# A planned attention and MoE kernel: key and query groups of four banks in place of six, with another list of ranks

## The chip, the cores and the metric

The kernel runs on one core of a Trainium2 chip. The metric is the device time of one execution in microseconds. Three runs of the kernel before took 358.09, 358.15 and 360.07, with a median of 358.15.

## What is computed

The reference is a linear attention with learned features, followed by a two-layer product with an ELU. Cut to what matters:

```python
def phi(x):                                   # x: 8 batches, 8 heads, 576 rows, 64 columns
    proj = x @ w_phi                          # 64 -> 128 features
    proj = proj - max(abs(proj), axis=-1)
    return concat([exp(proj), exp(-proj)])    # 256 features

q_p, k_p = phi(q), phi(k)
kv = einsum('bhsf,bhsd->bhfd', k_p, v);  z = sum(k_p, axis=2)
x = einsum('bhsf,bhfd->bhsd', q_p, kv) / (einsum('bhsf,bhf->bhs', q_p, z) + 1e-6)
x = x.transpose(0, 2, 1, 3).reshape(4608, 512)
h = x @ w_in                                  # 512 -> 2048
out = where(h > 0, h, exp(min(h, 0)) - 1) @ w_out   # 2048 -> 512
```

## The kernel before

**Tiling.** The attention works in 16 quads: quad `i` is half of batch `b = i // 2`, that is four heads. Of the 576 rows of a head, 512 are the main part and 64 the tail. For each quad TensorE projects the transposed keys and queries by `w_phi` (L689 for the main part, L671 for the tail), and projects the queries again with the features on the partitions (L864 and L876). The main projections contract over 64 rows only, so two heads run side by side on the two row halves of the array (`project_halves`, L689, and `queries_f`, L864). VectorE takes the largest absolute value of every row (L710), and ScalarE takes the exponentials straight from the projections (`EK` L757, `Eq` L944). GpSimd scales the values by the keys' weights (L808, L818). TensorE makes `kv` (L992) and the outputs (L1046, L1060, L1074). VectorE sums them (L1095, L1101) and GpSimd divides (L1143, L1172).

The MoE part works in nine chunks of 512 tokens. Chunk 0 needs quads 0 and 1; chunks 1 to 7 need two quads each; chunk 8 is made of all the tails. Each chunk has 16 first products (`ph`, L1354 in chunk 0, L1339 after), the ELU in three steps (ScalarE `e_sb` L1367, GpSimd `u_sb` L1371, VectorE `gT` L1383, the last of which reads `ph` again), and 16 second products (`po`, L1443), which are copied (L1471) and stored (L1480, L1484). The last pieces of chunk 8 are 256, 128 and 128 columns wide and share one buffer in SBUF.

**Order of the work.** The kernel is straight-line code, and a planner writes its order when the program is built. `plan_quad`, `plan_chunk` and `plan_loads` hand in operations with an estimated cost, what each depends on, and the PSUM banks that it takes (`new`) and reads (`uses`). There are eight banks, of four kinds: "first" for projections and transposes, "second" for `kv` and outputs, "ph" and "po" for the MoE part. `Planner.run` steps through a modelled time; each time an engine is free, it starts the ready operation with the lowest rank whose banks are free. The ranks stand in `RANKS`, two characters an operation, in the order in which the operations were handed in. An operation of mode 1 (the matmuls over 64 rows) after one of mode 0, or the reverse, costs a planned 0.095 us more (`CHANGE`). In the first 60 planned microseconds a gap of TensorE is half filled with matmuls on zeros (`fill`, L1651). What the chip runs is the resulting fixed order of each engine, with semaphores.

**Around the change.** For batches 4 to 7 (`b > MERGED`, `MERGED = 3`) the main keys and the first half of the first form of queries are one operation on TensorE: `keys` writes four banks of keys and two of queries. The other queries are one operation as well, `others`: the second half of the first form and both halves of the second form, six banks. For batches 1 to 3 keys are one operation of four banks, and for batches 2 and 3 each half of the queries is one operation of four banks (`both`). Quad 0 and 1 have smaller ones. In `run`, `first` is the lowest rank of the ready operations of more than four banks that don't find their banks free; no operation of a higher rank may take a bank ahead of it.

The queries of batch 0 are loaded in two halves by GpSimd (heads 0 to 3, heads 4 to 7), as are its keys and values; GpSimd also issues the loads of `w_in` (two) and `w_out` (four), and from quad 5 on SP issues the transposes of keys and queries by DMA.

Of the kernel before, what the change touches and what calls it, by code (L numbers as in the profile page):

```python
# [34 lines left out]
    "0t12141E1R1T8c1U1b6-1H1M1Q1Y1O1f1V1X1Z1k1m1q1u1g1v1r1i1x221tNx4iOS4-074Q7UBL0587"  # L35
    "4k6J2O5m2w2u5S2r2s5P2i2h5R2e2d5T2n2f2m2g1j1l1n251o47480A2A8KBQAx9591920b415A5B8G"
    "8E998z5D4o9698869B9ADU9RDS8J3z5t4M3X7J2t3c7H743o9M5EDV4w759t0p0n9z5i5h5u094F4R3+"
    "3w1+6N0J4Z066P0U8-04A+FHB0BP7l7mBJ8U7vBM7w8TBK7y7xBN8v7u8Y8Z612620272GAfAg3fDR5M"
    "586a6b6Z9kDQDNAKAJ9N8yAv8x5J4n90Aq9QAy97Aw2EB46f2o2q3k0O5p6C2p3v352J6QKM3t6FKN6W"
    "4K4IIu6l6rIt6q4T5H4e4Y4t0m2K2ZBR6OEy0200BZ5+7C3d5z6m4U7N3h3rAs4N9D0-6+7Q2F664u9y"  # L40
    "5W6I5G5o6S7dNk1h6x5F9v4DBd724G9L8n4d13DE931DAu4L4q107KAU446e0o3IA-5gC3EC235C3KC-"
    "7c0HBG55602YRGBD4jA69j3VE39C9V6BCH7P4EANEpC6DhD82XBUATFTFZ6tJl7L9s8b8iAZ4a2bAFB2"
    "7I1W4v4W9I1e4V8M3H338Q2D2C8L322x8F3834494J4H2+2y2P5Z5a5X5Y5c5b0y0r5v5w3Y3a3Z3b1c"
    "0w3B3A3l3i3m3j2v8f4g4f4h2cD42aDD534O9e3xBaAD1s0s0e3sBhBc5-8HBF363130ARClE1EW6R9+"
    "B57V2V9m4XCO01595l77715j7670659-736K9o786n2z39A29n8k1715161G8V8W2l3yABAC7GCL7FCK"
    "2-1a0v0u5e5Q5d5U3W0d0j0l0k54At689d9uDeE6AQEVDL4SBnBl9wE5DYAGDfCn6j1z1yGR4ABiAiFY"
    "3q63AMII1J6H0T5N1S4m1BGy0q691CGX8N8q198ICI037MAn9PJQ6pBw9l3n3EGoHHCD0xFt2WDWI5FF"
    "0f52JDBt6wAeID84Dz3-MDBC6g9rIAB67k6MFm4bF54lIEA5BxCMCFMiEEDHFsA7Ci0XB9FvGdCdDMEZ"
    "9F7-CV89FULg5r24212Q1-6i9S3J5V5q9g3e5k5n6G37ALBfB-C0BeD9CQBmCRCTBgDADCAO9K9JD6D7"
    "3C3G3D3F0c0i0h3pCkCjCgChCbCc406467CwC+CvCz5sBu9W9XCyAXBHBkC74z0+0BGW1F0C4y0E08Eb"  # L50
    "0g1ABj9xAP185x5yB7F4Co0aDT1d46ASAl8u8jAo8l8dAm8m8sAp8w8eDJCeCf8t8rA9626L6D6EA8AY"
    "4pCYBy1L1K1N1I4x6u6s9b9q9c9p6zAc8P8O2UEL6dEc8+BrIFIB8R454sBpKkHWBqH6MBBs42I4N32N"
    "2MBAB8GSMJEiHiEYPvAaH-EeEuFSVuCEWJC2ESCUWFB3ENCSW6BWGmCJTOBTIQCNBv94GgCPI34cETBO"
    "VQ6hHE7XVEF+Es51B17SAW3gEnK2VxDXW3EMWGD5U-DwVhD3ThC4VsDcEKDkD0S7IzDZEJDdFQVpJ3FO"
    "FMFIFgAbEkEFGpGqH19HEj5f6v3T6oAIEaAkEOMuJm5I4+0Z0K7j0V280N0W2H0L0Y0M0I0z1P0Q2I29"
    "Ds3SDm3Q3R3NDv5KGcGb7g7i7h825LGtGu8p8h7Y8BAr0P2L2T8o8aMl88IYEdGrNM7BQ3Ms7sH4Hq7r"
    "H3Ho7AQ2Mr505657AH1pJkJtG6F343CmMC6U6XNn6V7+Np808DMQ816T4r2S2R8C2B3U3L3MHZHa3P3O"
    "85TeTdRlM5M4Rj5OSfSgA1A3A4A09GFd7z7tRz7DNBC9LvBEJcEQBIOYEU7RJZGl7TFoGhCCJXERV+4C"
    "4B6kBSDjVLQCMyDFU0V-6cBbVqNRBV9OU+VNHTFVPeAERfFETWGCRTEPT1AhSzEGT2DbGTE9SFL5G3Ga"
    "TpIVI9FnSxFfH8GHRiAjI-FlGzFaIkFzJ-C1HsFkCGPtHnFi7EFXEDFwFxPIKVHgBzHNMFM6KZIZL9Hy"  # L60
    "KCMLPoKBFpEwGYEmJCLdGM0D0G3u0F0R0SDiBB9f9ECW7eWYWQWaWXWPWbWgWdWNWfWeWcMVNGNFWkWm"
    "W0WVWTWRWUWSWWWOWZ8XWMWLWoWiWKWhWpWsWqWrDOWjWlWnSQ9UTv9TVrF7SB79F9Rh7OF8HGRgF2HF"
    "7aF1HJ7bReCsCtD2Bo6Y8S6y7WDlCaVVV4V3VzV0W4VyUzV5VOV2VKVwW2W1W5VSV1L3L2L4L1VvVtW7"
    "VWEIDKDIWBWAVnW9W8VmWCWE7ZEHVeVgWHD-TwE0T3FLGEG5FNG4HdFyHhHzEzGkHfE8UpUwGGCpCqEX"
    "B+JLIPQIITJ7I8J6LqIaIjAVLQHlIqS6KKJVJgN6HQJRJaN0IHIXHOS5H+JHLbKSHVExO-KrJJEvPgKG"
    "MRG0QOOALWHbPULsSbGJQlHpStH5ULDgQKLIShMgRsKRHmLURwGKFBLaLnQQKYJBKcKaLcKlNtP9O1Oz"
    "PDGwJNHKP4KHMxMvJp6A2j1w2kJECZDqH2E4HPE7FPUZSrSsUPSqSnUOSoSmUaTUSy8AQzWITSTQJzJ+"
    "JuJwJxJyJvUQUNEoUqUoTmTlTqTrToUEUAUCD+83THTLU9GN7nGO7fJIIGG-GQGvI6HkCXKDIWJ4G+JK"
    "LoKnGLKTKUE+E-IvIoJ1DGHjFDGxIgIiHIIdJnISIfINHDIMIeGFTnU8JYIhS4KsKXKWL6N2N5H9HAGP"
    "G1G2GiGjGBGDGAG9G7G8FhHt7o7pIOEtMnFGQZHXSuRXFCM8SLLJRvSwLKRtUFGIS0UKDBFJFKKFJFKq"  # L70
    "UnNqPJOVTkRBR4KLSeTPMGK1SEUrLhK3JdTJMeK8M1SULlKAEqUJLiK0J2UTKhK9STU7LxHvTNPZO8Fu"
    "TIMHRpHrR2TZRqMwTGTKOZMXT8KOO5O0SWAzMKMqScPVSKFjPRRDNAS+RENLR8QqRIQ+GVMdJUJbNEQ0"
    "RkJqPGPEQTQRFrErBYC5BXKoUlDPCBAd7qDaI0TFNJP7TDPiPBTBP5PATCP6PhLtJfJjPnPmOBOJOKOI"
    "ONOCOMTETAF6U2U3P+PsPrQfQhQrQVQgElMNPkPjQWLMKdLLKmK5MtKyIJOLKPK7NoLZK4LpKwK+VDVX"
    "LyU6UUNlRMKtLPKuKpJhHYVoU4UgVfUmUfVaUhUbVcUdUeSpURUSTaVRTYTXUWUXUVUYU5VbVdHcViVj"
    "VZVYVMVGVHVJVIVFKbVBTMT-T7HSRrHURyKxRSRPKzRRSANIRQS2KeSOS8NHS1TfIL9Z9YLeGUP3JGGf"
    "QSNeQ69hN1QXJ5J0M7QsR-LfMUQmPOLuNyRAQjFRO2R1NQPyL-QuRKSRHCR6OWPFDnRUPqOUGZNYOyEf"
    "N9SjPlFeKiSdIsPCSHSkOmN8KESYNjNrR5OuPzOaFASlSaOtLFFbM+LELSLTNUHxRFNXNaNhNiOlRWOR"
    "OQOXOTIRMILBCuCACrOFQHFqF0FWFcHLLCV7UBT9V6T4T6VAUsTgVCUvT5RuUyUxU1R3TjTyTxTiTzUM"
    "T+V9V8IKVTVUTbTcTuUjUkTsTtUiNmUIVlVkKvMzSSMAUHImPWQaIlPSQbIpQGQdInQcQFJTQtRoQeEB"  # L80
    "EAHeGnNuO3LAKILVMhQpRdRnP1RcRYQoRNRaP2RmRZSJUGUDQLQMDxDuDpE2DtDrDyQnP0NDSXSZIwJ9"
    "IxJ8I+JAIyQ8NdQYQNQ5Q9N7SVN4ROQvMYNgRCM9LmR7MWMSQUMcMTQkMbMPDoEhEgPwPYI7NPRbM0K6"
    "SGL+PHLGI2OsLkLDRJJePuLRM3SNSPNWN+S9NOLXLrF-JsLjQJJiQ7NZIrLOM-NcMERLNvNVMoHRS3NT"
    "GeGsMaNbNCNsPxOOQiS-N-ODOrR0OvOPRHNSSiKgK-L0OeNNNwOdOxPbOiOnOqQDUtR9WDJrNKICI1HB"
    "IcRxPMKjLwPTLNOfOpO7UcOEQ4LYMmObNfJoSIOhQ-O4KQOcQAQBSCOgTRT0O9PaKfQxMMO+NzMpRVPd"
    "PpD1OGPcO6L8MfOwLzOjOHUuR+OkP8TTPLQEMOSvKJSDJSTVQPPQPXH0HMIUIbPfQw9aAAC8CxQyP-L7"
    "LHM2MjPPOoHuHwPKMZJMJOJPJWPNMk4P9i8g11Q1VPH7SM"
# [37 lines left out]
class Planner:  # L125
# [43 lines left out]
    def run(self):  # L169
# [8 lines left out]
        mode = 0  # L178
        pending = []
        landed = []  # L180
        DONE = len(self.ops)
# [55 lines left out]
        while todo:  # L237
            started = False
            for e in ready:
                if free[e] > now:  # L240
                    continue
                best = None
                first = min(
                    [o.rank for at, o in ready[e]
                     if at <= now and len(o.new) > 4 and not fits(o, e)],
                    default=DONE,
                )
                for at, o in ready[e]:
                    if at > now or o.engine or not fits(o, e):
                        continue  # L250
                    if o.new and o.rank > first:
                        continue

                    if any(
                        c < o.cost[e]
                        and free[x] <= now
                        and not any(a <= now and y is not o for a, y in ready[x])
                        for x, c in o.cost.items()
                    ):
                        continue  # L260
                    if best is None or o.rank < best.rank:
                        best = o
# [64 lines left out]
def kernel(  # L327
# [31 lines left out]
    MERGED = 3  # L359
# [162 lines left out]
    def plan_quad(i):  # L522
# [198 lines left out]
        for cs in ((0,), (1,), (2,)) if i == 0 else ((0, 1), (2,)):  # L721
            tail = cs == (2,)

            with_q = b > MERGED and not tail
            if with_q:
                q_first = [Bank("first") for _ in range(2)]

            def keys(e, cs=cs, with_q=with_q):
                for c in cs:
                    project_halves(0, range(4 * c, 4 * c + 4), main_banks[c])  # L730
                if with_q:
                    project_halves(1, range(4), q_first)

            new = [tail_bank] if tail else [x for c in cs for x in main_banks[c]]

            o = add(
                {"PE": 0.11 if tail else 0.22 * (len(cs) + with_q)},
# [3 lines left out]
                [moved[0][-1] if tail else moved[0][cs[0]], *old("kv"), landed["w_phi"]]  # L741
                + ([moved[1][0], *old("out")] if with_q else []),
                new=new + (q_first if with_q else []),
# [103 lines left out]
        exps_q = []  # L847
        m_qs = {0: [], 1: [], 2: []}
        for c in range(3):
# [4 lines left out]
            if b > MERGED and c == 0:  # L854
                pair = q_first
# [30 lines left out]
            if c < 2 and b > MERGED:  # L886
                if c == 0:
                    o, o_f = ops["k"][0], None
                    ops["q"].append(o)
                    rest = [(queries_f, pair_f)]  # L890
                else:
                    rest = [(queries, pair), *rest, (queries_f, pair_f)]

                    def others(e, rest=rest):
                        for f, _ in rest:
                            f(e)

                    o = o_f = add(
                        {"PE": 0.66}, others, deps,
                        new=[x for _, p in rest for x in p], mode=1, key=key,  # L900
                    )
            elif c < 2 and b > 1:
# [15 lines left out]
            if o_f:  # L918
                ops["q"] += [o] if o is o_f else [o, o_f]
# [768 lines left out]
```

## Time and profile before

| | us |
|---|---|
| median of three runs | 358.15 |
| the profiled execution | 358.15 |
| its span on the core | 356.4 |
| TensorE busy | 344.2 |
| VectorE busy | 264.4 |
| ScalarE busy | 261.6 |
| GpSimd busy | 243.5 |
| `po` L1443, 584 matmuls | 133.0 |
| `ph` L1339, 427 matmuls | 106.0 |
| main projections L689, keys and queries, 512 matmuls | 22.8 |
| second form of queries L864, 64 matmuls | 11.0 |
| fillers L1651, 132 matmuls | 12.9 |

The span is what the profiler saw on the core from the first instruction to the last, and the execution's time is a little longer. Matmuls are pipelined: a recorded duration overlaps the next one, so a price is better read from the distance between starts. A few per cent of the matmul records are missing. The granted clock of TensorE is full from 4 us to the end.

### The profile page before, as it was taken

What the parts mean: (1) busy time and instruction counts of PE and PEld (TensorE: products, weight loads), DVE (VectorE), ACT (ScalarE), POOL (GpSimd) and SP (SyncE); (2) the same over time, 40 slices, a digit from 0 to 9 for tenths busy, and PEclk for the clock granted to TensorE, in tenths of its full rate; (3) what the DMA queues carried; (4) which work ended last, traced back from release to release, by engine and by line L of the source; (5) the groups of instructions that cost most, each with busy time, mean ns of one, the idle gap of its engine ahead of it and who ended that gap; (6) DMA issues with size and microseconds to landing.
All of it is one profiled execution on the core that took longest, in us unless ns stands there. A gap on an engine that the chain in (4) does not pass through costs nothing.

```text
span 356.4 us, 9086 instructions
## 1 busy us (share of the span) xinstructions
PE 344.2 (97%) x3439; PEld 205.5 (58%) x3484; DVE 264.4 (74%) x571; ACT 261.6 (73%) x575; POOL 243.5 (68%) x342
## 2 busy tenths in 40 slices
PE   7899999999999999999999999999999999999995
PEld 6677779556654664565655565555656545454444
DVE  6999799989997899878879867985888744425300
ACT  5998988997779888788878788868677545445311
POOL 8899987979867896988736983599365844335200
PEclk9999999999999999999999999999999999999999
DMA  7999999995896896799847422622032110010023
GB/s 164 256 234 209 206 194 217 180 179 162 129 140 131 139 228 106 161 181 138 96 92 204 96 65 64 195 64 65 32 93 64 30 36 29 29 62 29 29 62 87
DMA packets 84268, 43.46 MB, mean 122 GB/s; under 512 B 54656, under 2 KB 77696, under 8 KB 84224
## 3 DMA queue, kind: packets, MB, share of 16 engines
q1 hardware_dynamic: 57632, 26.59, 32.6%
q0 software_dynamic: 25760, 15.47, 30.6%
q10 hardware_dynamic: 832, 0.82, 0.8%
q8 instruction: 27, 0.44, 0.5%
q14 instruction: 17, 0.14, 0.1%
HBM read 36.77 MB, written 9.44 MB: 130 GB/s over the span
## 4 chain that ended last, share of the span: by engine, by line
PE 85%; ACT 6%; DVE 3%; DMA 3%; issue 2%; POOL 1%; ACTq 0%; POOLq 0%
PE po L1443 32%; PE ph L1339 31%; PE pkv L992 5%; PE pk L689 4%; PE ph L1354 4%; PE pn L1046 3%; DMA t_b<-in_q_dram 3%; PE pq L864 2%; ACT Eq L944 2%; ACT EK L757 2%; DVE tot L1095 1%; PE pnt L1074 1%; DVE tot L1101 1%; ACT e_sb L1367 1%; PE pk L671 1%
## 5 line engine op out<-in xcount | busy, mean ns | idle before, releaser
L1443 PE MATMUL po<-w_out_sb,gT 128*128 128x512 bf16 (+2 forms) x584 | 133.0, 368 | 1.3 <-issue 0.2
L1371 POOL TENSOR_SCALAR u_sb<-e_sb 128x512 bf16<-128x512 f32 x144 | 88.5, 620 | 66.6 <-ACT e_sb L1367 62.8
L1383 DVE SCALAR_TENSOR_TENSOR gT<-u_sb,ph 128x512 bf16<-128x512 bf16 x144 | 96.1, 679 | 36.0 <-POOL u_sb L1371 35.7
L1367 ACT ACTIVATE e_sb<-ph 128x512 f32<-128x512 f32 x144 | 86.5, 613 | 38.2 <-PE ph L1339 31.5
L1339 PE MATMUL ph<-xT,w_in 128*128 128x512 bf16 x427 | 106.0, 380 | 1.8 <-DVE gT L1383 0.5
L1443 PEld LDWEIGHTS <-gT 128*128 128x128 bf16 x608 | 55.2, 98 | 58.3 <-issue 2.5
L1339 PEld LDWEIGHTS <-w_in 128*128 128x128 bf16 x512 | 54.5, 114 | 45.6 <-issue 3.0
L757 ACT ACTIVATE EK<-pk 128x512 bf16<-128x512 f32 x128 | 68.4, 630 | 7.5 <-PE pk L689 6.7
L944 ACT ACTIVATE Eq<-pq 128x512 bf16<-128x512 f32 x128 | 68.7, 638 | 5.6 <-PE pq L864 5.5
L808 POOL TENSOR_TENSOR vs<-v_b,em 128x512 bf16<-128x512 f32 x64 | 65.9, 1048 | 0.1
L710 DVE TENSOR_REDUCE m_q<-pk 128x4 f32<-128x512 f32 (+1 forms) x80 | 48.2, 629 | 10.5 <-PE pk L689 8.5
L710 DVE TENSOR_REDUCE m_k<-pk 128x4 f32<-128x512 f32 (+1 forms) x80 | 47.6, 626 | 4.7 <-PE pk L689 4.6
L1143 POOL TENSOR_TENSOR x<-tot,rec 128x576 bf16<-128x576 f32 x28 | 31.8, 1157 | 10.2 <-DVE rec L1139 10.0
L1471 ACT COPY o_sb<-po 128x512 f32<-128x512 f32 (+2 forms) x29 | 16.3, 561 | 30.6 <-PE po L1443 28.7
L1095 DVE TENSOR_TENSOR tot<-pn,w 128x260 f32<-128x260 f32 x64 | 26.6, 423 | 8.6 <-PE pn L1046 7.2
L1101 DVE TENSOR_TENSOR tot<-tot,pn 128x260 f32<-128x260 f32 x64 | 26.4, 419 | 0.5
L1046 PEld LDWEIGHTS <-Eq 128*128 128x128 bf16 x448 | 20.1, 97 | 9.1
L818 POOL TENSOR_TENSOR vst<-v_tail,em 128x260 bf16<-128x260 f32 x32 | 19.7, 624 | 7.2 <-ACT em L786 7.2
L1046 PE MATMUL pn<-kv,Eq 128*128 128x65 bf16 x448 | 21.9, 193 | 0.1
L992 PE MATMUL pkv<-vs,EK 128*128 128x65 bf16 x512 | 20.5, 194 | 0.0
L992 PEld LDWEIGHTS <-EK 128*128 128x128 bf16 x512 | 18.4, 98 | 2.9 <-DVE m_q L710 0.4
L1354 PE MATMUL ph<-xT,w_in 128*128 128x256 bf16 x128 | 17.6, 274 | 0.2 <-DVE xT L1266 0.2
(93 smaller groups left out, 315.3 us busy)
## 6 DMA issues: line engine op xcount, KB each, us to landing
out_dram<-o_sb SPq DMA_DIRECT2D x32, 256.0 KB, 2.4
v_b<-in_v_dram SPq DMA_DIRECT2D x6, 1024.0 KB, 5.6
k_b<-in_k_dram POOLq DMA_DIRECT2D x7, 512.0 KB, 8.0
q_b<-in_q_dram POOLq DMA_DIRECT2D x7, 512.0 KB, 8.7
w_out_sb<-in_moe_w_out_dram POOLq DMA_DIRECT2D x4, 512.0 KB, 17.5
w_in<-in_moe_w_in_dram POOLq DMA_DIRECT2D x2, 1024.0 KB, 18.8
v_b<-in_v_dram POOLq DMA_DIRECT2D x2, 512.0 KB, 8.6
v_b<-in_v_dram POOLq DMA_DIRECT2D x1, 1024.0 KB, 13.8
```

The costliest lines, as they stand in the source:

```text
L710: nc.vector.tensor_reduce(dst, src, axis=AX.X, op=ALU.max, apply_absolute_value=True)
L757: nc.scalar.activation(EK()[:, 2 * c + par, sg, :] if c < 2 else EKt[:, sg, :], bank.tile[:, 0:n, :].rearrange("p a b -> p (a b)"), ACT.Ex ...
L808: nc.gpsimd.tensor_tensor(st["vs"][:, sg, :, r, 0:D], kqv[b, 2][:, o:o + 2 * HW].rearrange("p (c n d) -> p c n d", c=2, d=D), by_head(st[" ...
L944: nc.scalar.activation(dst, src, ACT.Exp, scale=1.0 - 2.0 * sg)
L992: nc.tensor.matmul(pkv[:, c, sg, :], st["EK"][:, 2 * s + t % 2, sg, (2 * c + t // 2) * F:(2 * c + t // 2 + 1) * F,] if t < NT else EKt[:, ...
L1046: nc.tensor.matmul(pt[:, t, :], st["Eq"][:, par, s, sg, o:o + P], st["kv"][:, s, c, sg, :], start=True, stop=True,)
L1339: nc.tensor.matmul(ph, w_in_of(ct, jt), xTs[ch][:, ct, :] if ch < B else xT_tail[:, ct // 2, :, ct % 2, :], start=(ct == 0), stop=(ct == N ...
L1354: nc.tensor.matmul(bank.tile[:, j, :], w_in_of(ct, jt + j), xTs[ch][:, ct, hf * CHUNK // 2:(hf + 1) * CHUNK // 2], start=(j == 0 and ct == 0),
L1367: nc.scalar.activation(t["e"], flat(bank.tile), ACT.Exp)
L1371: nc.gpsimd.tensor_scalar(t["u"], t["e"], -1.0, 1.0, op0=ALU.add, op1=ALU.mult)
L1383: nc.vector.scalar_tensor_tensor(dst, u, 0.0, bank.tile, op0=ALU.min, op1=ALU.max)
L1443: nc.tensor.matmul(bank.tile, gTs[ch][:, jt, tt * P:(tt + 1) * P], w_out_sb[:, jt, o0:o1], start=(jt == 0), stop=(jt == N_JT - 1),)
```

## The change

Three things differ.

1. `MERGED`, `with_q`, `q_first`, `others` and `exps_q` are gone. Batches 4 to 7 get the form of batches 2 and 3: one operation for the main keys (four banks), and two operations `both` for the queries (four banks each: half of the first form, half of the second form). The exponentials of a half of the queries now depend on that half's operation. The keys' operation no longer depends on the transposed queries and on the outputs of the quad two before.
2. `first` is gone from `Planner.run`.
3. `RANKS` is another list, of 2111 entries in place of 2103.

The description of the change speaks of a last output piece of 128 columns with a shared buffer; these lines are the same in both kernels. It also says that the new ranks were searched with a doubled price on idle stretches of TensorE in the ramp.

```diff
-    "0t12141E1R1T8c1U1b6-1H1M1Q1Y1O1f1V1X1Z1k1m1q1u1g1v1r1i1x221tNx4iOS4-074Q7UBL0587"
...
+    "020305040A098x0B0CR+06070E0G080D0K0F0I0M0P0R0Z0L0o0X0N0b0y0YEd4kJp5G12OnCrWD2MV-"
...
-        DONE = len(self.ops)
...
-                first = min(
-                    [o.rank for at, o in ready[e]
-                     if at <= now and len(o.new) > 4 and not fits(o, e)],
-                    default=DONE,
-                )
                 for at, o in ready[e]:
                     if at > now or o.engine or not fits(o, e):
                         continue
-                    if o.new and o.rank > first:
-                        continue
...
-    MERGED = 3
...
-            with_q = b > MERGED and not tail
-            if with_q:
-                q_first = [Bank("first") for _ in range(2)]
-
-            def keys(e, cs=cs, with_q=with_q):
+            def keys(e, cs=cs):
                 for c in cs:
                     project_halves(0, range(4 * c, 4 * c + 4), main_banks[c])
-                if with_q:
-                    project_halves(1, range(4), q_first)
...
-                {"PE": 0.11 if tail else 0.22 * (len(cs) + with_q)},
+                {"PE": 0.11 if tail else 0.22 * len(cs)},
...
-                [moved[0][-1] if tail else moved[0][cs[0]], *old("kv"), landed["w_phi"]]
-                + ([moved[1][0], *old("out")] if with_q else []),
-                new=new + (q_first if with_q else []),
+                [moved[0][-1] if tail else moved[0][cs[0]], *old("kv"), landed["w_phi"]],
+                new=[tail_bank] if tail else [x for c in cs for x in main_banks[c]],
...
-            if c < 2 and b > MERGED:
-                if c == 0:
-                    o, o_f = ops["k"][0], None
-                    ops["q"].append(o)
-                    rest = [(queries_f, pair_f)]
-                else:
-                    rest = [(queries, pair), *rest, (queries_f, pair_f)]
-
-                    def others(e, rest=rest):
-                        for f, _ in rest:
-                            f(e)
-
-                    o = o_f = add(
-                        {"PE": 0.66}, others, deps,
-                        new=[x for _, p in rest for x in p], mode=1, key=key,
-                    )
-            elif c < 2 and b > 1:
+            if c < 2 and b > 1:
 
                 def both(e, first=queries, then=queries_f):
                     first(e)
                     then(e)
 
                 o = o_f = add(
                     {"PE": 0.44}, both, deps, new=pair + pair_f, mode=1, key=key
                 )
```

## The prediction

> **What bounds the kernel now.** I read the page first, then the busy time by stretches of 10 us, then TensorE's timeline around the groups that the change splits, then TensorE's waits.
>
> From the page, busy shares, slices and the chain that ended last:
>
> ```profile
> PE 344.2 (97%) x3439; PEld 205.5 (58%) x3484; DVE 264.4 (74%) x571; ACT 261.6 (73%) x575; POOL 243.5 (68%) x342
> PE   7899999999999999999999999999999999999995
> PE 85%; ACT 6%; DVE 3%; DMA 3%; issue 2%; POOL 1%; ACTq 0%; POOLq 0%
> ```
>
> TensorE is at 97% and makes 85% of the chain. A busy TensorE may still be doing filler work, so the stretches come next (columns: TensorE, weight loads, VectorE, ScalarE, GpSimd, each with its instructions, then clock, DMA share, GB/s):
>
> ```profile
> 10.00:20.00 10.00, 8.51 (x141) 6.32 (x139) 9.47 (x19) 9.90 (x29) 9.19 (x14) 1.00 1.26 274
> 20.00:30.00 10.00, 9.42 (x201) 7.37 (x200) 9.36 (x28) 9.89 (x31) 9.96 (x16) 1.00 1.21 205
> 30.00:40.00 10.00, 9.53 (x143) 8.11 (x142) 7.48 (x25) 8.89 (x20) 9.96 (x15) 1.00 1.16 213
> ```
>
> In the ramp ScalarE is the full engine: 9.90 and 9.89 of 10. TensorE is filled up there. The same view for the filler tile alone (columns: TensorE busy, clock, DMA share, GB/s):
>
> ```profile
> 4.36:10.00 5.64, 1.96 (x23) 1.00 1.10 197
> 10.00:20.00 10.00, 4.14 (x47) 1.00 1.26 274
> 20.00:33.37 13.37, 2.99 (x27) 1.00 1.21 207
> ```
>
> So between the first real transpose (4.36) and the first product of chunk 0 (33.37), 97 fillers, 9.1 us as recorded, stand where no work was ready. After that TensorE waits for almost nothing. Its waits from 36 to 352 us are, in full:
>
> ```profile
> PE ph L1339 <- DVE gT L1383: 0.5, 1, 0.5
> PE ph L1354 <- DVE xT L1266: 0.2, 1, 0.2
> PE po L1443 <- issue: 0.2, 1, 0.2
> ```
>
> Two laws follow. From 33 us on, whatever adds TensorE time adds as much to the end. Before that, the end moves only if ScalarE delivers earlier or later.
>
> **Part 1: six-bank groups become four-bank groups.** For batches 4 to 7 (eight quads) the old order projects keys and the first queries in one visit, and the rest of the queries in a second. The new one has keys, queries c=0 and queries c=1, three visits. The matmuls are the same: 16 key matmuls and 8 + 8 query matmuls on L689, 2 + 2 on L864. What changes is how often TensorE goes from 128-row to 64-row matmuls and back. The timeline of TensorE has the price; a merged visit:
>
> ```profile
> 140.62 2.75 PE L1443 MATMUL po<-w_out_sb,gT 128*128 128x512 bf16 x12
> 143.31 0.62 PE L689 MATMUL pk<-w_phi_both,kT 64*128 64x128 bf16 x16
> 143.76 0.39 PE L689 MATMUL pk<-w_phi_both,qT 64*128 64x128 bf16 x8
> 144.08 1.90 PE L1443 MATMUL po<-w_out_sb,gT 128*128 128x512 bf16 x8
> ```
>
> Twelve matmuls of 512 columns take 12 x 0.216 = 2.59 us (0.216 is the step from one start to the next, 0.86 per 4 in the chain), so the work is over at 140.62 + 2.59 = 143.21 and the visit starts at 143.31: 0.10 us to go in. Its 24 matmuls run in 12 pairs on the two halves of the array, 0.056 us a pair (the step of the 128-column transposes): 0.67 us. It lasts 144.08 - 143.31 = 0.77, so 0.10 to come out. In the starts to the nanosecond, 312 ns stand between a 512-column matmul and a visit where 216 stand otherwise: 96 ns a crossing, **0.19 us a visit**.
>
> In the trace batches 4 to 7 make 16 such visits (from 122 to 264 us). Three per quad make 24: 8 x 0.19 = **+1.53 us**, all of it on the path, since it lies after 33 us. Two visits that stand next to each other save one price. Batches 2 and 3 already have the three-visit form: 12 visits from 63 to 118 us, none back to back with another. I allow at most two joins (-0.4) and take none.
>
> The skill has a rule for this price. The Trainium skill's TensorEngine Tiling (Array Packing), section Key Properties, says that changing the tiling mode drains the array; TensorE: Matmul & The Clock Gate, in the phase DRAIN, puts a drain at about 128 cycles. An estimate from these, 128 / 2.4 GHz = 53 ns a crossing, would make +0.85 us of the eight visits. The row, 96 ns, decides.
>
> **What the split gives back.** Six banks of eight for a visit leave two for the MoE products. The one long wait above shows what this costs; TensorE again:
>
> ```profile
> 134.22 0.62 PE L689 MATMUL pk<-w_phi_both,kT 64*128 64x128 bf16 x16
> 134.70 0.40 PE L689 MATMUL pk<-w_phi_both,qT 64*128 64x128 bf16 x8
> 135.64 2.98 PE L1339 MATMUL ph<-xT,w_in 128*128 128x512 bf16 x12 [0.55 <-DVE gT L1383]
> ```
>
> The next ph needs a bank that VectorE's ELU still reads. With four banks taken, four are left, and this 0.55 us can go. The other 15 visits have no such wait, so 0.55 is all there is to gain. Against it stands the new order's own luck: I bound new bank waits by none and by two of this size (+1.1), and take 0 for the sum of both.
>
> The keys no longer wait for the transposed queries. TensorE shows no wait on keys after 36 us, so that gains nothing. The wait added is that of a four-bank visit for banks. Queued behind it in TensorE's fixed order are the MoE products, and ScalarE's e_sb after those. Its nearest row is the same 0.55. Reductions (L710, 0.63 us) and exponentials (L944, 0.64) stay the same in number; VectorE and ScalarE are 74% and 73% busy and cover their new places. The planner's `first` rule drops out with the only ops of more than four banks: no instruction.
>
> **Part 2: all ranks are new.** Each rank list is a permutation (2103 old, 2111 new), and names of ops cannot be put in order of time from it alone, except where all ops are ready from the start: GpSimd's first loads. There the queries of heads 4 to 7 of batch 0 move from behind the first queries to behind the keys of batch 1, and the query tails come one place earlier. In the trace one such issue takes 0.74 to 0.95 us on GpSimd, so the tails start about 0.75 earlier (TensorE waited 0.39 for them at 15.54) and heads 4 to 7 about three places, 2.4 us, later. They landed about 8 us after their issue at 4.6 and are transposed at 14.55; they would be there at 15 or, behind 1 MB more, about 17. ScalarE is busy with quad 0 until about 21 us, which covers it; uncovered it would cost up to 2.4. The weights w_in keep the number of loads before them.
>
> For the rest of the ramp I bound by ScalarE. It idles 0.2 us of 10 to 30 and 1.1 us of 30 to 40, so a better order gains at most **1.3 us**. A worse one loses what ScalarE's larger gaps show, 1.23 and 0.85 before its casts and first exponentials: **+2.1**. Without a sign for either I take 0, the ScalarE rows of 10 to 30 being nearest to full.
>
> The last output piece of 128 columns, which the change's description names, isn't in the diff: before copies 128x128 pieces at 351.81 and 352.70 already. It costs nothing either way.
>
> **Sum.** The profiled execution took 358.15 with a span of 356.4, 1.75 around it, and is the median of the runs. 358.15 + 1.53 + 0 + 0 = **359.7 us**.
>
> **Rivals.** (a) *The new ranks win more than the visits cost*, not slower than before. Place: 10 to 40 us, ScalarE. Price: -1.3 there and -0.55 at the bank wait, so 358.15 + 1.53 - 1.85 = 357.8. It decides once ScalarE finishes quads 0 and 1 over 1.5 us earlier, some 27 fillers of 56 ns fewer than 97. For it: 97 fillers are left to win from. Against it: ScalarE has little idle time left. (b) *A worse order*: 2.1 us in the ramp and two bank waits, 358.15 + 1.53 + 2.1 + 1.1 = 362.9; half of it 361.3. For it: ranks are tuned for a plan, not for the chip, and the old plan meets the chip with only 0.9 us of waits; there is more to lose than to win. (c) *The visits are joined*: the plan puts them back to back, the count stays at 16 to 18, and the time is 358.2 to 358.6. Against it: batches 2 and 3.
>
> **How the numbers follow.** Forecast (359.0 to 360.6) 0.5; (a) 0.17; (b) from 360.6 up 0.23; (c) 0.1. The low end is (a)'s 357.8. At the upper end I leave out the last tenth of (b), and stop at 362.3. A measurement of this kernel tells about 1%, 3.6 us, from no change: above 361.7 lies about half of (b), 0.12; below 354.6 nothing here leads, 0.02; within, 0.86.
>
> **What would show it.** Right: 24 visits on L689/L864 for batches 4 to 7, each with 312 ns into it after a 512-column matmul; no wait of ph for gT behind a visit; first L1354 near 33.4. Wrong: first L1354 moved by more than 1 us, fillers far from 97, visits back to back, or TensorE idle of over 1 us after 36 us. A wait on a load in the first 20 us would undo the argument on the queries of heads 4 to 7.

## The result and the profile after

The changed kernel takes 360.58 us, the median of 20 executions (360.02 to 362.27). The kernel before takes 358.39 beside it (20 executions, 357.98 to 360.07). The ratio is **1.0058**, with a 95% interval of 1.0045 to 1.0070: 2.2 us slower, a small difference that the interval shows all the same, and inside the 1% that the prediction took for the least that a measurement tells from no change. The forecast was 359.7 in a range of 357.8 to 362.3.

The profiled execution of the changed kernel took 360.80 with a span of 359.0. Against the 358.15 of the one before that is 2.65 us more. From its page, busy shares, slices (TensorE, then its granted clock) and the chain that ended last:

```profile
PE 346.8 (97%) x3436; PEld 206.2 (57%) x3484; DVE 267.2 (74%) x576; ACT 258.5 (72%) x570; POOL 243.8 (68%) x342
...
PE   7898999999999999999999999999999999999995
...
PEclk9899999999999999999999999999999999999999
...
PE 86%; DVE 4%; ACT 3%; DMA 2%; POOL 1%; issue 1%; ACTq 0%; SPq 0%; POOLq 0%
```

The bound is where it was: TensorE, 97% busy, 86% of the chain. In the rows shown two digits are new: in the second slice the clock is an 8, and in the fourth TensorE is an 8 in place of a 9. The busy time by stretches of 10 us (columns: TensorE, weight loads, VectorE, ScalarE, GpSimd, each with its instructions, then clock, DMA share, GB/s) shows the same place:

```profile
10.00:20.00 10.00, 8.45 (x117) 6.24 (x116) 8.09 (x16) 9.62 (x29) 8.67 (x12) 0.83 1.30 271
20.00:30.00 10.00, 9.78 (x217) 7.90 (x216) 9.63 (x28) 9.40 (x24) 9.78 (x15) 1.00 1.18 205
30.00:40.00 10.00, 9.01 (x138) 7.27 (x135) 8.86 (x29) 8.37 (x19) 9.62 (x15) 1.00 1.17 212
```

The mean clock from 10 to 20 us is 0.83 where it was 1.00. ScalarE, nearly full before (9.90 and 9.89 from 10 to 30), is now at 9.62 and 9.40: it waits in this execution, but not in one at full clock (the part on the prediction has the rows). The filler tile alone, in the stretches of the prediction (TensorE busy, clock, DMA share, GB/s):

```profile
4.36:10.00 5.64, 2.78 (x29) 1.00 1.11 196
10.00:20.00 10.00, 3.33 (x31) 0.83 1.30 271
20.00:33.37 13.37, 3.34 (x39) 1.00 1.19 205
```

99 fillers against 97: the same number, moved from the middle stretch to the outer ones. The visits of batches 4 to 7, in TensorE's timeline, look as forecast: the two halves of the queries are visits of their own.

```profile
148.12 0.40 PE L680 MATMUL pk<-w_phi_both,qT 64*128 64x128 bf16 x8
148.36 0.38 PE L843 MATMUL pq<-qT,w_phi_both 64*128 64x512 bf16 x2
148.67 1.90 PE L1400 MATMUL po<-w_out_sb,gT 128*128 128x512 bf16 x8
150.50 0.40 PE L680 MATMUL pk<-w_phi_both,qT 64*128 64x128 bf16 x8
150.74 0.38 PE L843 MATMUL pq<-qT,w_phi_both 64*128 64x512 bf16 x2
```

And TensorE's waits from 36 to 354 us, in full (total, times, longest):

```profile
PE ph L1296 <- DMA xT<-x: 0.7, 1, 0.7
PE po L1400 <- issue: 0.5, 3, 0.2
PE ph L1296 <- issue: 0.2, 1, 0.2
```

The wait of a first product for a bank (0.5 for `gT`) is gone. In its place one of 0.7 for a transpose by DMA stands, at 257.35.

**An account of TensorE.** Some matmul records are missing from any trace, but the weight loads are all there, one for each matmul. I priced each by the step from start to start that its shape has where nothing waits (0.216 us for 512 columns, 0.056 for 128), added 0.192 for each visit to the projections over 64 rows, and called the rest "lost": waits, fillers, and matmuls at half clock. The split at 60 us separates the ramp.

| us | end of TensorE | visits | lost up to 60 | lost after 60 |
|---|---|---|---|---|
| before | 352.46 | 47 | 15.94 | 3.28 |
| after | 355.10 | 56 | 17.01 | 3.17 |
| difference | +2.64 | 9 x 0.192 = +1.73 | +1.07 | -0.11 |

So 1.54 us are the eight visits of batches 4 to 7 (24 in place of 16), 1.3 are the ramp (one visit more, 0.19, and 1.07 lost), and the late waits cancel. The three parts make 2.69 where the ends lie 2.64 apart, so the account is good to about 0.05. It doesn't count the transposes of tails over 64 rows as visits; one of them stands alone before, two after, so some 0.2 of the 1.07 is one more way in and out. The experiments test each of the three.

### The profile page after: what moved, and what is told of

The parts are those of the page before. It is cut to its first block, busy times and chain, and to the rows that moved or that the text cites. A ratio compares the mean times of both kernels' runs of the same rounds, so it can differ in the third digit from the quotient of the medians.

```text
span 359.0 us, 9085 instructions
## 1 busy us (share of the span) xinstructions
PE 346.8 (97%) x3436; PEld 206.2 (57%) x3484; DVE 267.2 (74%) x576; ACT 258.5 (72%) x570; POOL 243.8 (68%) x342
## 4 chain that ended last, share of the span: by engine, by line
PE 86%; DVE 4%; ACT 3%; DMA 2%; POOL 1%; issue 1%; ACTq 0%; SPq 0%; POOLq 0%
PE po L1400 34%; PE ph L1296 28%; PE pk L680 5%; PE pkv L949 5%; PE ph L1311 4%; PE pn L1003 3%; PE pq L843 2%; ACT EK L739 2%; DMA xT<-x 1%; PE pnt L1031 1%; DMA v_b<-in_k_dram 1%; PE tr L619 1%; DVE tot L1052 1%; PE pk L662 1%; DVE tot L1058 1%
## 5 line engine op out<-in xcount | busy, mean ns | idle before, releaser
L1400 PEld LDWEIGHTS <-gT 128*128 128x128 bf16 x608 | 54.4, 98 | 57.0 <-issue 2.9
L701 DVE TENSOR_REDUCE m_q<-pk 128x4 f32<-128x512 f32 (+1 forms) x80 | 47.4, 628 | 9.8 <-PE pk L680 9.6
L1428 ACT COPY o_sb<-po 128x512 f32<-128x512 f32 (+2 forms) x26 | 14.6, 562 | 24.9 <-PE po L1400 24.7
```

What stands on the lines that cost most here:

```text
L701: nc.vector.tensor_reduce(dst, src, axis=AX.X, op=ALU.max, apply_absolute_value=True)
L1400: nc.tensor.matmul(bank.tile, gTs[ch][:, jt, tt * P:(tt + 1) * P], w_out_sb[:, jt, o0:o1], start=(jt == 0), stop=(jt == N_JT - 1),)
```

## The experiments

The kernel before is run beside each of them; its medians were 358.36, 358.38 and 358.38.

### The price of a visit

The kernel before with each of the 16 merged visits of batches 4 to 7 broken in two by a matmul on zeros over 128 rows, and, as its control, the same kind of matmuls without a break. Both do extra work whose result nothing reads.

```diff
# split16
             def keys(...):
...
                 if with_q:
+                    nc.tensor.matmul(psum(q_first[0], [P, P], FP32, "pad"), zeros, zeros, ...)
                     project_halves(1, range(4), q_first)
...
                     def others(e, rest=rest):
-                        for f, _ in rest:
-                            f(e)
+                        for n, (f, p) in enumerate(rest):
+                            if n == 1:
+                                nc.tensor.matmul(psum(p[0], [P, P], FP32, "pad"), zeros, zeros, ...)
+                            f(e)
# pad16, ahead of the tail queries' projection (128-row matmuls on both sides)
+                if b > MERGED:
+                    pad = psum(pair[0], [P, 2, P], FP32, "pad")
+                    for n in range(2):
+                        nc.tensor.matmul(pad[:, n, :], zeros, zeros, ...)
```

> The kernel before, in its own order. Each of the 16 merged visits of batches 4 to 7 is broken once by one matmul of 128 columns on zeros over all 128 rows, so there are 16 visits more and 16 matmuls of 0.056 us more. If a visit costs 0.19 us wherever it stands: 16 x (0.19 + 0.056) = +4.0, 362.4 us. Rival, that TensorE has slack around the visits which hides the crossing: only the matmuls, +0.9, 359.3, or nothing.

> The kernel before, in its own order, with the same 16 zero matmuls put where TensorE is in the 128-row mode anyway (two ahead of each tail projection of the queries of batches 4 to 7). No visit is added. If TensorE sets the end, +0.9, 359.3 us; split16 minus this is the price of 16 visits, 3.1 us by the rows. Rival, slack: 358.4.

Measured: split16 365.26 (ratio 1.0170, 1.0138 to 1.0202), pad16 362.64 (1.0112, 1.0069 to 1.0154). Both are about 3 us above every expectation, so neither says what a visit costs. TensorE's timeline of pad16 shows why, here at two places:

```profile
140.76 0.28 PE L876 MATMUL pad<-zeros 128*128 128x128 bf16 x2
141.09 0.27 PE L671 MATMUL pk<-w_phi_both,qT 128*128 128x256 bf16 x1
...
290.08 3.18 PE L1345 MATMUL ph<-xT,w_in 128*128 128x512 bf16 x14 [0.92 <-DMA xT<-x]
```

Two 128-column matmuls should be over 0.11 us after 140.76, but `pk` starts 0.33 after it, just behind the recorded end of the pads (141.04). The pad was a tile of its own in `pk`'s bank, and the bank was handed from one tile to the next: 0.22 us at each of the eight places, 1.8 in all, which I had not priced. In split16 such a break takes 0.28 us from the zeros to the next matmul where the step and a crossing make 0.15: 0.13 more at each of 16 places, 2.1 in all. The rest is in the last row: in both kernels one wait of 0.9 for a transposed `x` is new. The pair was run again with the zeros written to the very tile that the real matmuls then overwrite, four at a time:

```diff
+        def pad(tile):
+            for n in range(4):
+                nc.tensor.matmul(tile[:, n * P:(n + 1) * P], zeros, zeros, ...)
# split16b
             def project_halves(n, blocks, pair, padded=False):
+            if padded:
+                pad(pk[0].rearrange("p a b -> p (a b)"))
# ... the same on pq in queries_f where it is the second part of `others`
# pad16b
             def project(n, hh, bank, pads=0):
+            for _ in range(pads):
+                pad(pk.rearrange("p a b -> p (a b)"))
```

> The first pair of padded kernels paid for more than the visits, because the pad was a tile of its own in the bank and TensorE waited for it to end. Here the pad lies in the tile that is then written, and is four zero matmuls of 128 columns (0.22 us, as long as one of 512 columns, so that the next weights load behind it). The kernel before, its own order, 16 merged visits broken once each: 64 x 0.056 + 16 x 0.19 = 3.6 + 3.1 = +6.6, 365.0 us. In the trace 96 ns into and out of each broken visit. Rival, slack: as the control.

> The control: the same 64 zero matmuls ahead of the tail projections of the queries of batches 4 to 7, in the tile that they write, no visit added. +3.6, 361.9 us; the difference from split16b is 16 visits, 3.1 us by the rows. Rival, slack hides them: 358.4. A wait of ph for the transposed x, as the first pair showed, may add up to 0.9 to either.

Measured: split16b 364.87 (1.0187, 1.0157 to 1.0216), pad16b **361.91** (1.0102, 1.0075 to 1.0129). The control is 3.53 above the kernel before; its 64 zero matmuls of 0.0556 make 3.56. So pads cost what their columns cost, and the break is the difference: (364.87 - 361.91) / 16 = **0.185 us a visit** (medians of four executions each). One of the breaks in split16b's timeline:

```profile
143.65 0.62 PE L697 MATMUL pk<-w_phi_both,kT 64*128 64x128 bf16 x16
144.21 0.40 PE L683 MATMUL pk<-zeros 128*128 128x128 bf16 x4
144.53 0.40 PE L697 MATMUL pk<-w_phi_both,qT 64*128 64x128 bf16 x8
```

The 16 key matmuls run in 8 pairs, 0.45 us; the zeros start 0.56 after them, 0.11 later than that. Four zeros take 0.22; the queries start 0.32 after, 0.10 later. The prediction's 0.19 a visit stands, measured in the time of the whole kernel.

### Where the 2.2 us lie

Two kernels, each with one half of the change in it. The first has the four-bank groups, runs in the order of the kernel before up to 102 planned us, and then in that of the changed kernel. The second has the six-bank groups, the order of the changed kernel up to 46 planned us, and that of before from there.

```diff
# h_before100, from the changed kernel
-RANKS = (the changed kernel's)
+RANKS = (the order that the kernel before executes up to 102 planned us, then the changed kernel's)
# h_after40, from the kernel before
-RANKS = (the kernel before's)
+RANKS = (the order that the changed kernel executes up to 46 planned us, then the kernel before's)
```

> The four-bank groups of the changed kernel, with ranks that keep the order of the kernel before up to 102 planned us and the order of the changed kernel's ranks after it. If the visits cost 1.5 us and the ramp of the changed kernel the rest: 358.4 + 1.5 - 0.55 (the bank wait) + 0 to 0.7 (new waits) = 359.4 to 360.0 us, first product of chunk 0 at 33.4. Rival, all of the 2.2 us comes with the four-bank groups and their late order: 360.6.

> The six-bank groups of the kernel before, with ranks that keep the order of the changed kernel up to 46 planned us and the order of the ranks of before after it. If the ramp of the changed kernel costs 0.7 to 1.2 us: 359.1 to 359.6 us, and the granted clock is half for some us between 15 and 20 in a part of the executions. Rival, the ramp costs nothing: 358.4.

Measured: h_before100 360.02 (1.0030, 1.0012 to 1.0048), h_after40 359.16 (1.0013, 0.9991 to 1.0034). The late part (the groups with their order) gives +1.7, of which the eight visits are 1.54; the ramp alone gives +0.8. They add up to 2.5 against the 2.2 of both. The interval of the second reaches down to no change, and three of its executions took 358.34 to 358.44, as short as before, so the time doesn't prove the ramp's part. The account of its profiled execution (358.87) has it: 0.69 more lost up to 60 us than before, and one visit more, 48. Its TensorE reaches the first product of chunk 0 a microsecond late:

```profile
33.08 0.40 PE L1259 MATMUL tr<-ident,x 128*128 128x128 bf16 x4 [0.95 <-POOL x L1172]
33.31 0.41 PE L1060 MATMUL pn<-kv,Eq 128*128 128x65 bf16 x8
33.56 1.06 PE L628 MATMUL tr<-ident,q_b 128*128 128x128 bf16 x16
34.45 1.26 PE L1354 MATMUL ph<-xT,w_in 128*128 128x256 bf16 x10
```

The transposes of `x` wait 0.95 for GpSimd's division of the attention outputs, and then 16 transposes of queries, nearly 0.9 us, stand ahead of the first product. It starts at 34.45 (34.63 in the changed kernel, 33.37 before), with no half clock in the ramp of this execution.

### The groups without the new order

The four-bank groups with the order of before all the way: where two operations of six banks stood, three of four banks stand.

```diff
# s4_oldranks, from the changed kernel
-RANKS = (the changed kernel's)
+RANKS = (the order that the kernel before executes; the first half of the queries right behind the keys)
```

> Part 1 alone: the four-bank groups with the ranks of before, no new search; the queries c=0 stand right behind the keys, c=1 where the second merged visit stood. If the rank list and the form of the groups belong together, keys and queries c=0 ask for eight banks nearly at once, TensorE waits several tenths in most of the eight quads, and the time is over 361 us. Rival, the list carries over and only the visits less the bank wait count: 359.3.

Measured: 361.72 (1.0092, 1.0074 to 1.0109), the slowest of the four mixtures. It has 55 visits, so keys and first queries, next to each other in the rank list, do not join on the chip; the planner starts the lowest rank whose banks are free, and passes over one that finds none. After 60 us it loses 5.01 us where before and after lose 3.2. The time is the one expected, over 361, but the reason given for it holds only in part: TensorE does not wait in most of the eight quads. Two of the 24 visits are held up by more than 0.1 us (by 0.8 and 0.45), and a few other matmuls by 0.2 to 0.4. The longer one, in TensorE's timeline:

```profile
140.62 0.66 PE L680 MATMUL pk<-w_phi_both,qT 64*128 64x128 bf16 x8
141.34 0.71 PE L843 MATMUL pq<-qT,w_phi_both 64*128 64x512 bf16 x2
141.98 0.82 PE L1400 MATMUL po<-w_out_sb,gT 128*128 128x512 bf16 x3
```

It lasts 1.36 where the visit at 148.12 of the changed kernel lasts 0.55. So the new ranks are worth something: 1.8 us of later waits that the new groups have in the old order are gone in the new one.

### The wait for the transposed x

In the changed kernel the only wait of more than 0.2 us after 36 us is this one, from TensorE's timeline:

```profile
255.19 1.46 PE L1296 MATMUL ph<-xT,w_in 128*128 128x512 bf16 x6
257.35 0.59 PE L1296 MATMUL ph<-xT,w_in 128*128 128x512 bf16 x2 [0.71 <-DMA xT<-x]
```

It was 0.9 in h_before100 and 1.1 in a_again, the changed kernel's other profile below. The plan expects those transposes earlier than they land. A later planned landing for this one quad puts 5 of TensorE's 536 operations into another order near 254 us, and leaves everything else in its place. The same was done to h_before100.

```diff
# a_xt33 from the changed kernel, h_b100_xt33 from h_before100
-                {"SP": 1.27}, x_by_dma, ops["x"] + prior, key=-6.0, load=0.7, alone=1.85
+                {"SP": 1.27}, x_by_dma, ops["x"] + prior, key=-6.0, load=0.7,
+                alone=3.3 if i == 13 else 1.85
# and RANKS = the order executed without the edit
```

> The changed kernel with one planned cost changed: the transposed x of quad 13 is planned to land 3.3 us after its issue in place of 1.85, with the order otherwise held. TensorE then does one group of outputs and the keys' visit of quad 15 before the first ph of the next chunk (five operations of 536 change places, near 254 us). If the wait of ph for that transpose (0.7 in the changed kernel's trace, 0.9 in h_before100's) is a cost of its own: -0.5 to -0.9, 359.7 to 360.0 us, no wait of ph for the transpose left over 0.2. Rival, it comes back as another wait: 360.5.

> h_before100 (ramp of before, four-bank groups after 102 planned us) with the same one cost changed. What is left against before is then 8 visits at 0.19 less the bank wait of 0.55: 358.4 + 1.5 - 0.55 = 359.3 us, 0.7 below h_before100. Rival, the wait comes back elsewhere: 360.0.

Measured: a_xt33 360.37 (1.0054, 1.0040 to 1.0068), h_b100_xt33 360.04 (1.0049, 1.0032 to 1.0066). The rival held both times: the wait goes and the time stays. The same stretch of a_xt33:

```profile
255.54 0.41 PE L1003 MATMUL pn<-kv,Eq 128*128 128x65 bf16 x8
255.88 1.20 PE L680 MATMUL pk<-w_phi_both,kT 64*128 64x128 bf16 x16
257.29 1.52 PE L1296 MATMUL ph<-xT,w_in 128*128 128x512 bf16 x6 [0.21 <-DVE gT L1340]
```

A visit of keys, moved up into the gap, takes 1.41 us until the next start where 0.55 is usual (such a visit is recorded with 0.62); the last 0.21 of it is a wait for a bank. That is all of what had been 0.71. What holds the visit up is VectorE, in its timeline:

```profile
255.88 0.43 DVE L1058 TENSOR_TENSOR tot<-tot,pn 128x260 f32<-128x260 f32 x1
256.22 0.42 DVE L1052 TENSOR_TENSOR tot<-pn,w 128x260 f32<-128x260 f32 x1
```

Half of the keys' matmuls start at 255.88; the next ones start at 256.36 and 256.70, each 0.05 us after one of these sums of the outputs `pn` ends, and each waits for VectorE's semaphore. So the transpose wasn't the only thing late: the banks that the keys take came free no sooner. Over all, the account of a_xt33 has 3.32 lost after 60 us, against 3.17 in the changed kernel.

### The clock in the ramp and the fillers

The changed kernel's profile had half clock from 15.83 to 19.25 us. Two kernels change how much of a planned gap is filled with matmuls on zeros, from a half to a quarter and to 0.9; the third is the changed kernel, unchanged, for its clock in another execution.

```diff
# b_fill25 and b_fill90, from the kernel before
-                    n = int(0.5 * (now - max(free[e], banks[filled])) / self.FILL)
+                    n = int(0.25 * (now - max(free[e], banks[filled])) / self.FILL)   # 0.9 in b_fill90
```

> The kernel before, its own order, with a quarter of each planned gap of TensorE filled in the ramp in place of half. In the runs so far the executions of before at a mean granted clock of 0.995 took about 1 us more than those at 0.998 to 1.0, and those at 0.989 about 2.5 us. If fewer fillers let the clock fall to half more often, most executions are at 0.990 to 0.995 and the median is 359.3 to 361. Rival, the clock has nothing to do with the fillers: 358.4 and the same mix of clocks.

> The kernel before, its own order, with 0.9 of each planned gap filled. If the fillers keep the clock up: all executions at 0.998 to 1.0 and 358.2 to 358.5 us, without those of 359 to 361 that before has. Rival, fillers stand in the way of work that is ready earlier than planned: over 358.5 in all of them.

> The changed kernel unchanged, for a second trace. If the half clock between 15.8 and 19.3 us was the cause of most of its lag in the ramp, a trace without it has the first product of chunk 0 at 33.6 or before. If the order in the ramp is the cause, it is at 34.3 or later without it too, as in h_after40.

Measured: b_fill25 359.58 (1.0028, 1.0016 to 1.0039) and b_fill90 359.46 (1.0023, 1.0011 to 1.0036). With 76 fillers in all in place of 132, 7 of 12 executions show a mean clock of 0.988 to 0.995, and the profiled one ran at half clock for two stretches on end:

```profile
4.36:10.00 5.64, 1.52 (x10) 0.79 1.12 199
10.00:20.00 10.00, 2.88 (x19) 0.78 1.26 275
```

(The filler tile of b_fill25, columns as above.) But its executions with a mean clock of 1.000 took 359.6 to 360.05, no less than the others. Why it is 1.2 us slower stays open; the clock isn't ruled out by this, since a mean of 1.000 can hide a late start at full clock, as a_again shows below. With 0.9 filled, all 12 executions keep a clock of 0.998 or more, and the kernel is 1.1 us slower all the same: here the rival held, fillers that stand in the way of real work. The filler tile of b_fill90:

```profile
10.00:20.00 10.00, 5.99 (x83) 1.00 1.26 277
20.00:33.37 13.37, 5.11 (x62) 1.00 1.20 205
```

145 fillers from 10 us on where there were 74, and the first product of chunk 0 starts at 34.95 in place of 33.37.

The changed kernel, executed once more (a_again), took 361.76, and its first product starts at 35.16. TensorE waits 1.51 there for the first keys (0.61 in the other profile), and up to 13.1 us its matmuls take nearly twice their time. Here are eight transposes in a_again's timeline, then eight in the changed kernel's first profile:

```profile
10.81 1.06 PE L619 MATMUL tr<-ident,k_b 128*128 128x128 bf16 x8
```

```profile
8.92 0.61 PE L619 MATMUL tr<-ident,k_b 128*128 128x128 bf16 x8
```

The view says clock 1.00 for both. But the clock's records begin only at 13.13 us in a_again, and at 5.59 in the first profile, and ahead of its first record a profile shows 1.00. So a 1.00 there, or a mean clock of 1.000, doesn't prove a full clock, and this execution can't separate order from clock. What can are the two profiles in which neither sign of a half clock shows: a_xt33, whose ramp is the changed kernel's, with the first product at 34.07 and 16.40 lost up to 60 us; and h_after40, with 34.45 and 16.63. Before has 33.37 and 15.94. So in these two profiles **the order of the ramp costs 0.5 to 0.7 us**, and the half clock another 0.4 to 0.6 of the 17.01 in the changed kernel's first profile. Of the two values named ahead of a_again, 33.6 and 34.3, neither is met by 34.07: both causes have a part. The medians agree with the first of these: of their 2.19 the visits take 1.73 and the later waits give back 0.11, which leaves 0.57. The second part belongs to the execution that was profiled; 13 of the 20 have a mean clock of 0.998 or more, with a median of 360.48.

## Why the prediction was right

**The time.** 359.7 was forecast, 360.58 measured: inside the range and the 1%, 0.9 above the number. That is the upper end of the likeliest case (359.0 to 360.6), and nearly all of the 0.9 is the ramp.

**The visits** (+1.53): right. There are 24 in batches 4 to 7, none joined; in the starts to the nanosecond 312 ns stand between a 512-column matmul and a visit, as before; and 0.185 us a visit was measured apart from everything else. The rival (c), joined visits, fell. The estimate of 53 ns a crossing, from the Trainium skill's TensorEngine Tiling (Array Packing), Key Properties, and TensorE: Matmul & The Clock Gate, phase DRAIN, would have given +0.85; half of the measured 0.185 is 92 ns, so the trace's row was the one to take.

**The bank wait** (-0.55, against 0 to +1.1 of new ones, sum 0): right in its sum, in part by luck. The wait for `gT` at 135.64 is gone, as the four free banks let one expect. A wait of 0.71 came, but not for a bank: for a transpose by DMA, whose landing the prediction hadn't looked at. That the two nearly cancel followed from no reason given. Lost time after 60 us went from 3.28 to 3.17. Taking the new wait away gained nothing either, as VectorE's sums then hold the keys' banks. The wait of a four-bank visit for banks, priced at 0.55, came up in the old order (0.8 and 0.45 in s4_oldranks) and not in the new one.

**GpSimd's first loads**: right, with nothing to spare. The query tails are issued at 5.34 in place of 6.05, and TensorE's wait of 0.4 for them is gone. The queries of heads 4 to 7 are issued at 6.80 in place of 4.57, and TensorE waits for no load between 4 and 36 us in this profile. But they landed at 18.60, not at about 17, and TensorE, late by its half clock, came to them at 19.48. In the two profiles whose ramp runs at full clock their transposes start 0.05 us after the landing (18.91 and 18.96 in a_xt33, 18.25 and 18.30 in h_after40), and in a_xt33 TensorE waits 0.41 for the keys of batch 1, which landed at 17.52. A wait on a load in the first 20 us was the prediction's sign against this argument; there it came, for the keys and not for the queries that it named.

**The rest of the ramp** (taken as 0 between -1.3 and +2.1): this is the step that failed, the term that was mis-sized. The account has +1.07 and one visit more, 0.19. Part of it is order, +0.5 to +0.7 by a_xt33 and h_after40, and the prediction's own sign for it, a first product of chunk 0 more than 1 us from 33.4, came up: it starts at 34.63. The prediction bounded the ramp by ScalarE's idle time: the end moves only if ScalarE delivers earlier or later. That reading failed. At full clock the new order leaves ScalarE about as full as before, when it was at 9.90 and 9.89 of 10, and the first product is late all the same. From 10 to 30 us, a_xt33 and then h_after40:

```profile
10.00:20.00 10.00, 8.03 (x128) 5.83 (x126) 8.98 (x18) 9.85 (x31) 8.46 (x11) 1.00 1.29 271
20.00:30.00 10.00, 9.55 (x215) 7.80 (x214) 9.63 (x28) 9.90 (x26) 9.96 (x16) 1.00 1.18 205
...
10.00:20.00 10.00, 8.30 (x138) 6.09 (x137) 9.31 (x19) 10.00 (x31) 9.11 (x13) 1.00 1.29 268
20.00:30.00 10.00, 9.53 (x209) 7.69 (x204) 9.70 (x29) 10.00 (x27) 9.57 (x15) 1.00 1.18 205
```

How full an engine is doesn't say which work it does first. In h_after40 TensorE's waits for GpSimd's `x` grow from 0.5 to 1.2, as much as its ramp loses; in a_xt33 no single wait does, and what its order loses was not taken apart. In the changed kernel's own profile ScalarE stands still at 20.48 for a projection of queries that TensorE delivers late (ScalarE's timeline, with its idle time in brackets):

```profile
20.48 2.06 ACT L906 ACTIVATE Eq<-pq 128x512 bf16<-128x512 f32 x4 [0.86 <-PE pq L843]
```

And the transposes of `x`, the last step ahead of chunk 0, wait 0.83 for `EK`, where before they waited 0.3 at most for GpSimd's `x` (the row of before from TensorE's waits, 4 to 36 us, then TensorE's timeline after):

```profile
PE tr L1259 <- POOL x L1172: 0.5, 2, 0.3
...
31.28 0.22 PE L1200 MATMUL trt<-ident,x 128*128 128x128 bf16 x1 [0.83 <-ACT EK L739]
```

Both waits are mostly the half clock's: in a_xt33 ScalarE idles only 0.15 at that place, and the wait for `EK` is 0.3. That is the other part, and the prediction left it out: it priced TensorE in the ramp at full clock, and this execution has half. TensorE's timeline shows eight transposes taking 1.03 us there, and TensorE's clock by stretches (columns as in the view by 10 us) the two rows around it:

```profile
17.36 1.03 PE L619 MATMUL tr<-ident,k_b 128*128 128x128 bf16 x8
```

```profile
15.80:17.50 1.70, 1.70 (x12) 0.80 (x12) 1.62 (x3) 1.70 (x7) 1.18 (x2) 0.51 1.29 307
17.50:19.20 1.70, 1.70 (x22) 1.47 (x21) 0.69 (x1) 1.70 (x7) 1.58 (x3) 0.50 1.08 365
```

Later, at full clock, eight such transposes take 0.61 (19.48). These 3.4 us lie just ahead of the gap of ScalarE at 20.48, whose releaser is TensorE.

**The number of fillers** was named as a sign of the ramp, and it failed as one: 99 against 97, and the ramp 1.3 us worse. Half of each planned gap is filled, so fillers count the plan's gaps, not the chip's losses, and they don't stand where the chip had no work ready, as the prediction read them.

**The rivals.** (a), the ramp wins more than the visits cost, fell: the first product came later, not earlier. (b), a worse order, held for the ramp alone, with 1.26 of its 2.1 us in the profile (0.57 and a visit in the medians), and without its bank waits. The sum of the forecast with the measured ramp, 358.15 + 1.53 - 0.11 + 1.26, is 360.8, which is what the profiled execution took, within the 0.05 of the account.

## What to carry to other kernels

Where one engine is full from end to end, count how often the edit makes it change its mode and multiply by a price read from two starts: that term held to a hundredth of a microsecond a visit here, while "no sign known, so 0" for a reordered ramp was off by 1.3. A rank list belongs to the operations that it was searched for: the new groups lost 1.8 us more in the old order, and even with their own ranks they are slower than the old groups. And a wait taken from a full engine is only a gain if nothing behind it is just as late: here a wait of 0.7 us and one of 0.9 were removed with no gain that the runs show.

## What the runs showed of the chip

**Half clock comes in pieces of 3.4 us.** In the ramps of these kernels TensorE's granted clock is recorded as 0.5 for 3413 ns (15.83 to 19.25 us in the changed kernel, 8.73 to 12.15 in h_before100, 8.04 to 11.45 in h_b100_xt33, 8.19 to 11.60 in s4_oldranks) and for 6827 ns, twice that, in b_fill25 (7.60 to 14.43). The stretches at full clock between two changes fit the same step: 10240 ns ahead of the drop in the changed kernel are three, and 341333 ns behind it a hundred. The Trainium skill's TensorE: Matmul & The Clock Gate, under What's actually happening, describes free-running windows of 3413 ns; the stretches agree with that length. How busy TensorE is in a window doesn't decide alone: in the changed kernel it is busy for 2.44 us from 12.41 to 15.83 and the clock then drops, in pad16 for 2.15 from 12.28 to 15.70, a window of its own records, and the clock stays full. What decides no run here shows. The page's advice against idle gaps of TensorE over some 3 us, under Why this matters for your kernels, wasn't enough here: the longest gap from 6.2 us to the drop is 0.58.

**A bank handed from one tile to another costs TensorE 0.22 us**, even if both are written by TensorE and nobody reads the first: 0.33 from pad to `pk` in pad16 in place of 0.11, since `pk` starts only when the pads' recorded time is over. Where the handover meets a change between 128-row and 64-row matmuls (split16) it adds 0.13. With the zeros in the same tile (pad16b) the cost is that of their columns, 3.53 us for 64.
